# A new order for the steps of a fused retention and SwiGLU kernel, from its second up stage to its end

## The chip, the cores and the metric

The kernel runs on one core of one Trainium2 chip. The metric is the device time of one execution in microseconds; the time of a kernel is the median of several runs. TensorE (PE in the profile) multiplies, with its weight loads listed apart (PEld); VectorE (DVE), ScalarE (ACT) and GpSimd (POOL) do the elementwise work; SyncE (SP) issues nearly all transfers. Each engine works through its own list of instructions in order and waits on semaphores for the others.

## What is computed

A retention layer (a recurrent form of attention with a decay per head), and behind it a SwiGLU feed-forward block on its output. The sizes are 4 sequences, 8 heads, 768 steps, 64 elements per head, so 3072 tokens of 512 elements; the feed-forward width is 1536. All is float32.

```python
for t in range(S):                       # per sequence and head
    state = gamma * state + outer(k[:, :, t], v[:, :, t])
    y[:, :, t] = scale * (q[:, :, t] @ state)
x = y.transpose(0, 2, 1, 3).reshape(B * S, H * D)
g = x @ w_gate
out = (silu(g) * (x @ w_val)) @ w_out
```

## The kernel before

The tokens go through in four segments, numbered 0 to 3, of 2 x 384 tokens each. A segment has an up stage (x times w_gate and w_val, and the gate) and a down stage (the gated values times w_out). While segment s is in its stages, the retention of segment s+1 is done between the products, in chunks, as many small products of 64 rows and columns: `mm`, line 824, called from `scores_of` (or `scores_of1`), `low`, `old` and `grow`.

Precision: each float32 operand is split into three pieces that TensorE takes in its fast float32 form. The first piece is made on ScalarE, the second on VectorE, the third on GpSimd or VectorE; one block of products is then a series over the pieces.

The up stages 1 to 3 (`up3`, `product`, line 1229) use a scheme of Strassen's kind: for each of the 12 blocks f of the width, seven products p0 to p6 of six matmuls of 384 columns each, in four banks of PSUM, and ten small steps u0 to u9 between them that copy a bank out (u0, u3, u4 on ScalarE, lines 1244 to 1246), add (VectorE, lines 1244 to 1247) and apply the gate. A product that adds to a bank must wait until a step has taken out what it held: p2 of a block waits for u0.

The down stages (`down`, line 1298) have 12 blocks of six products, one for each 128 tokens, each of three matmuls of 512 columns. The weights of a block (`w_load`, line 1277, tile oitem, 768 KB) come into one of three slots, so a load can be issued only when the block three places ahead is through.

The retention of a segment goes by pairs p = 0, 1, 2 of chunks. The inputs come with `load_pair` (lines 815 and 819; one such load is up to four transfers). The scores go into banks, VectorE multiplies them with the decay mask (line 846), ScalarE scales k with the decays (line 857), TensorE mixes (`mix2`), ScalarE copies the results out into chunk_x (line 1159), and VectorE adds the new state to the old (line 923).

The order of all this is written out by hand in one list, `PLAN` (lines 51 to 235): each word is a step, with the number of the segment ahead of the slash. `run` calls the steps in this order, and since each step emits its instructions when it is called, the list fixes the order on every engine and in every queue. The names that the prediction uses:

- s/pF.N product N of block F in the up stage of segment s; s/uF.N its small steps
- s/wF.G.K piece K (0 on ScalarE, 1 on VectorE, 2 on GpSimd or VectorE) of group G of the weights of block F
- s/WF load of the down weights of block F; s/DF.T down product for tokens T; s/eT and s/oT its closing copy and store
- s/lN load N of the retention's inputs (5 to a pair: k, q, v and k, q by rows); s/scP scores of pair P; s/AP and s/BP the two mixings of pair P; s/kP.N scaling of k; s/yP.ZR copies of results; s/newP.Z adding to the state

The set `ELSE` (lines 236 to 245) names the steps that go to the other engine than usual: a third piece of weights (line 1134) goes to VectorE if it is in the set and to GpSimd if not, and a closing copy e changes between ScalarE and VectorE (lines 1327 and 1329).

```python
def run():
    for key in PLAN.split():
        if key in events:
            events.pop(key)[2]()
        else:
            do(key)
...
def either(step):
    return both if step in ELSE else pool
```

Of the kernel before, what the change touches and what calls it, by code (L numbers as in the profile page):

```python
# [113 lines left out]
    1/w3.2.0 1/u2.0 1/p2.2 1/u2.3 1/w1.2.2 1/p1.6 1/w3.0.1 1/w2.2.2 1/u2.1 1/w3.0.2 1/L4 0/o1 1/u1.8
    0/o4 2/tc 1/L5 1/p2.3 1/p2.4 1/u2.4 1/p2.5 0/e3 0/e5 2/tb 1/w4.1.0 1/w4.0.0 1/w3.2.1
    1/u1.9 1/p3.0 1/u3.0 1/w3.1.1 2/R 1/L6 1/u2.5 1/p2.6 1/u2.6 1/u1.2 1/w3.1.2 1/p3.3 1/u3.4
    1/u2.8 1/w4.0.1 1/u2.9 1/w4.0.2 1/u1.7 1/p3.2 1/u3.3 1/w4.1.1 1/p3.1 1/u3.1 1/p4.0 1/p3.4 1/p3.5
    1/w4.1.2 1/u3.6 1/u3.5 1/p4.1 1/w5.1.0 1/w5.1.1 1/u4.0 1/p4.2 1/w5.0.0 1/w4.2.0 1/w5.2.0 1/w5.2.1 1/w5.2.2
    1/w4.2.1 1/p4.3 1/u4.3 1/p4.4 1/w5.0.1 1/u2.2 1/u4.4 1/w3.2.2 1/p3.6 1/w6.2.0 1/p4.5 1/u3.8 1/u4.5
    1/u2.7 1/w6.1.0 1/w4.2.2 1/w6.0.0 1/p4.6 1/u4.8 1/u3.9 1/w5.0.2 1/p5.0 1/u3.2 1/u4.1 1/u4.2 1/u5.0  # L120
    1/p5.1 1/u4.6 1/p5.2 1/w5.1.2 1/p5.3 1/u5.3 1/u5.4 1/p5.4 1/L7 0/o5 2/l0 1/p5.5 1/w7.1.0
    1/w7.0.0 1/w6.1.1 1/w6.0.1 1/u4.9 1/u5.1 1/u4.7 1/u3.7 1/w6.2.1 1/u5.5 1/u5.6 1/w6.2.2 2/cv1 1/w7.0.1
    1/w6.0.2 1/p6.0 1/p5.6 1/u6.0 2/cv3 1/u5.8 1/u5.9 1/p6.1 1/u6.1 1/w7.1.1 1/p6.2 1/w6.1.2 1/p6.3
    1/L8 1/w7.2.0 1/u6.3 1/p6.4 1/L9 1/u6.4 1/u6.5 2/td 1/w8.2.0 1/p6.5 1/w8.1.0 1/w8.0.0 1/p6.6
    1/u6.8 0/o3 1/w7.0.2 1/w7.1.2 1/u6.6 1/p7.3 1/u7.4 1/u5.2 1/u6.2 1/w8.2.1 1/w7.2.1 1/L10 1/w8.2.2
    1/w8.0.1 1/u6.9 1/w8.1.1 1/p7.0 1/u7.0 1/p7.1 1/u7.1 1/u5.7 1/p7.2 1/u7.3 1/w8.0.2 1/p8.0 1/u8.0
    1/u7.2 1/w9.2.0 1/p7.4 1/p7.5 1/u7.6 1/w9.1.0 1/w9.0.0 1/p8.1 1/u8.1 1/w9.2.1 1/u7.5 1/w9.0.1 1/w9.1.1
    1/p8.2 1/w8.1.2 1/p8.3 2/cv0 1/u8.3 1/u8.4 1/w7.2.2 1/p7.6 1/u7.8 1/u7.9 1/w10.2.0 1/L11 2/l3
    2/k0.2 2/k0.0 1/p8.5 1/p8.4 1/w10.2.1 1/u8.5 1/w9.1.2 1/w10.1.0 1/w9.0.2 1/p9.0 1/u9.0 1/w10.0.0 1/p9.1
    1/w10.1.1 1/u8.6 1/w9.2.2 1/u7.7 1/w10.0.1 1/w10.0.2 1/p8.6 1/w11.2.0 2/k0.3 1/p9.2 1/u9.3 1/u8.8 1/w11.2.1  # L130
    1/w11.2.2 1/w10.2.2 2/l1 2/sc0 2/l6 1/p9.3 1/u9.4 1/p9.4 1/p9.5 1/w11.1.0 1/w11.0.0 2/cv2 2/dec0.1
    1/u8.9 1/u9.5 1/p9.6 1/u9.1 1/u6.7 1/u9.2 1/u9.6 2/l4 1/p10.0 1/w11.0.1 1/w11.0.2 1/w11.1.1 1/W0
    2/l2 1/u9.8 2/k0.1 1/u10.0 2/l10 2/l5 1/w10.1.2 1/w11.1.2 1/u9.9 1/p10.1 1/p10.3 1/u10.4 1/p10.2
    1/u8.2 1/u10.3 1/p10.5 1/p10.4 1/h0.0 1/u10.6 2/q0.0 1/p11.3 1/p11.0 1/h1.0 1/u10.5 1/p10.6 1/h0.1
    1/u10.1 1/h0.2 1/u9.7 1/u11.0 1/p11.2 1/p11.1 1/u10.8 1/u11.3 1/u11.4 1/p11.4 1/h1.1 2/l9 1/u10.9
    1/p11.5 1/u11.1 1/u8.7 1/u10.2 1/u11.2 1/u11.5 1/p11.6 1/u11.6 1/D0.1 1/u10.7 2/dec0.0 1/D0.2 1/u11.8
    1/u11.9 2/A0 2/new0.0 2/sc1 1/h1.2 1/u11.7 1/D0.3 1/W1 1/D1.3 1/D1.1 2/dec1.0 2/dec1.1 1/D0.4
    1/D0.5 1/D0.0 1/D1.5 1/D1.0 2/cm 2/was0.10 2/mv0.0 2/was0.11 2/y0.01 1/h2.0 1/h4.0 1/h2.1 2/y0.00
# [11 lines left out]
    1/W9 1/h11.0 2/L0 1/D8.4 1/D8.5 2/new2.0 2/mv2.0 2/was2.11 2/x1.0.2 1/h9.2 1/D9.2 2/x1.0.1 1/h11.1  # L150
    1/h11.2 2/y2.00 2/was2.10 2/B2 2/y2.10 2/sum2.2 2/y2.11 2/sum2.0 2/sum2.1 1/D9.1 1/D9.4 1/D9.5 1/W10
    1/D9.0 1/D10.1 1/D9.3 1/W11 1/D11.1 1/D10.3 1/D10.4 2/L2 1/D10.2 1/D10.5 1/D11.4 1/D10.0 1/D11.5
    2/w0.0.0 2/w0.0.1 2/sum2.3 2/x2.1.0 2/new2.1 2/w0.0.2 2/x2.0.0 2/x2.0.2 3/was0.01 2/x2.1.1 2/w0.1.0 2/w0.2.0 2/x2.2.0
    2/x2.2.1 2/x2.2.2 2/w0.2.1 2/x2.0.1 2/x2.1.2 2/w0.1.1 2/L3 2/w0.1.2 1/D11.0 1/e0 2/w1.0.0 2/w1.0.1 1/e1
    1/o1 2/w1.2.0 2/w1.2.1 2/w1.2.2 1/o0 1/D11.2 1/D11.3 2/p0.0 2/u0.0 2/w1.1.0 2/p0.1 2/w0.2.2 2/w1.1.1
    2/w1.1.2 2/L4 2/p0.2 2/u0.3 2/w2.1.0 2/p0.3 2/p0.4 2/u0.4 2/p0.5 2/w2.0.0 2/u0.1 2/u0.5 1/e2
    2/w1.0.2 2/w2.0.1 2/p0.6 2/u0.8 2/u0.9 2/w2.0.2 2/p1.0 2/u1.0 2/p1.1 2/p1.2 2/u0.6 2/p2.0 2/p1.3
    2/w3.1.0 2/w3.1.1 2/u1.1 2/w2.1.1 2/u1.3 2/p1.4 2/w2.2.0 2/u2.0 2/w2.2.1 2/p2.1 1/e3 2/w3.2.0 2/u1.4
    2/u1.5 2/p1.5 2/u1.6 2/w2.2.2 2/u0.2 2/w3.0.0 2/w3.0.1 2/u0.7 2/p2.2 2/u2.3 2/p1.6 2/u1.8 2/u1.9
    2/w2.1.2 2/w3.0.2 2/p2.3 2/u2.4 2/p2.4 2/p2.5 2/w4.1.0 2/w4.0.0 2/u2.1 2/u2.5 2/p2.6 2/u2.8 2/u2.6  # L160
    2/w4.0.1 2/w4.0.2 2/u2.9 2/w4.2.0 2/p3.0 2/u3.0 2/p3.1 2/w4.1.1 2/w4.1.2 2/L5 2/p3.2 2/u1.2 2/u3.3
    2/u3.1 2/w3.1.2 2/p3.3 2/u2.2 2/p3.4 2/u3.4 2/p3.5 2/w5.1.0 2/w5.2.0 2/u1.7 2/w3.2.1 2/w3.2.2 2/u3.5
    2/w5.2.1 2/w5.2.2 2/p4.0 2/u4.0 2/u3.2 2/w5.1.1 2/w4.2.1 2/p3.6 2/u3.8 2/w5.0.0 2/w5.1.2 2/p4.1 2/L6
    2/p4.2 2/u3.6 2/u3.9 2/u4.3 2/p4.3 2/u4.4 2/p4.4 2/p4.5 2/w6.1.0 2/w5.0.1 2/u4.1 2/w5.0.2 2/p5.0
    2/u5.0 2/u4.6 2/u4.5 2/p5.3 2/w6.2.0 2/u5.4 2/w6.1.1 2/p5.1 2/p5.2 1/e4 2/w6.0.0 2/w6.0.1 2/u5.1
    2/L7 2/p5.5 2/u5.3 2/u5.6 2/p5.4 2/w7.1.0 2/w4.2.2 2/p4.6 2/w7.2.0 2/u4.8 2/w7.0.0 2/w6.1.2 2/u5.5
    2/w7.2.1 2/u3.7 2/u5.2 2/u4.9 2/u2.7 2/u4.2 2/w6.2.1 2/u5.7 2/p5.6 2/u5.8 2/w6.0.2 2/p6.1 2/p6.0
    2/u6.0 2/p6.3 1/o3 2/u6.4 2/p6.2 2/u6.3 2/p6.5 2/L8 1/o2 3/l3 3/k0.0 2/L9 2/p6.4
    2/w6.2.2 2/u4.7 2/w7.0.1 2/w7.0.2 2/u5.9 2/p7.0 2/w7.1.1 2/L10 2/u6.5 2/u6.6 1/e5 2/w8.2.0 1/o5
    2/w8.2.1 2/u6.1 2/w8.1.0 2/w8.0.0 2/w8.0.1 2/w8.1.1 2/L11 1/o4 3/l0 2/w8.2.2 2/mv2.1 2/u7.0 2/p6.6  # L170
    2/w7.1.2 2/p7.3 2/u7.4 2/p7.2 2/u7.3 2/p7.5 2/u7.6 2/u6.8 2/u6.9 2/u6.2 2/p7.1 2/p7.4 2/w9.1.0
    2/w9.0.0 2/w9.2.0 2/u7.5 2/w8.0.2 2/p8.0 2/u7.1 2/u8.0 2/w9.0.1 2/w9.1.1 2/w9.1.2 3/l1 2/w9.0.2 2/w9.2.1
    2/w7.2.2 2/p7.6 2/u7.8 2/w8.1.2 2/p8.3 2/p8.2 2/u8.4 2/p8.5 2/u8.3 2/u8.6 2/p8.4 3/k0.3 2/w10.1.0
    2/u6.7 2/u8.5 2/p9.3 2/u9.4 2/u7.2 2/u7.9 2/p8.1 2/p9.0 2/p8.6 2/u8.1 2/u9.0 2/p9.2 2/u7.7
    2/w10.0.0 2/w10.0.1 2/u8.8 2/w10.1.1 3/l4 2/w10.0.2 2/u8.9 2/p9.5 2/p9.1 2/u9.3 2/p9.4 3/k0.1 2/p10.0
# [1319 lines left out]
```

## Time and profile before

| | us |
|---|---|
| median of three runs | 640.45 |
| lowest and highest run | 640.33, 642.25 |
| the profiled execution | 641.82 |
| its span, first to last instruction | 639.95 |

The profile is of one further execution. Its span is the time between the first and the last instruction on the core, and 1.87 us of its time lie around that. In the views, a row of a timeline has its start, its length, engine, line, operation, output and inputs and the number of instructions, and behind them in brackets how long the engine was idle before and what released it; "issue" is time in which the profile shows nothing that the engine waited for. The rows of stretches have for each engine its busy time and in brackets its number of instructions. Queue 8 carries TensorE's instructions into the core, in packets. The granted clock of TensorE is 1.00 in every stretch but the last.

The stages lie in the span like this: the first up stage to about 105 us, the down stages of segments 0, 1 and 2 from about 105 to 196, 286 to 347 and 437 to 500 us, the up stages of segments 1, 2 and 3 between and behind them, and the last down stage from about 587 us.

### The profile page before, as it was taken

The numbers are of one execution on the slowest core, as the hardware profiler recorded it, in microseconds if no ns is written. First come the engines' busy times: TensorE is split into PE (matmuls) and PEld (weight loads), VectorE is DVE, ScalarE is ACT, GpSimd is POOL, SyncE is SP. The second block draws the span as 40 slices with busy tenths as digits, with TensorE's granted clock in tenths as the row PEclk, the third lists the DMA queues.
The fourth block names the chain that finished last, engine by engine and source line by source line (L and its number), as shares of the span: only waits on it lengthen the run. The fifth ranks groups of instructions, "written<-read, shape, count | busy, mean of one in ns | idle before, by whom it ended". The sixth has DMA issues, their size and how long they took to land.

```text
span 639.9 us, 14128 instructions
## 1 busy us (share of the span) xinstructions
PE 632.4 (99%) x5587; PEld 582.4 (91%) x5587; DVE 502.3 (78%) x759; ACT 397.2 (62%) x845; POOL 181.8 (28%) x121
## 2 busy tenths in 40 slices
...
GB/s 319 276 347 332 366 319 277 276 319 304 257 283 304 181 148 188 144 249 218 295 239 182 129 125 188 198 189 192 240 376 168 166 115 116 178 32 145 214 197 149
DMA packets 57747, 143.03 MB, mean 224 GB/s; under 512 B 5840, under 2 KB 28368, under 8 KB 57680
## 3 DMA queue, kind: packets, MB, share of 16 engines
...
q8 instruction: 44, 0.72, 0.5%
...
## 4 chain that ended last, share of the span: by engine, by line
PE 92%; DMA 3%; ACT 3%; issue 1%; DVE 1%; SPq 0%; ACTq 0%
PE bank L1229 40%; PE bank L1298 28%; PE bank L1056 13%; PE bank L824 5%; PE bank L1074 3%; DMA hT<-in_k_n_dram 2%; PE bank L650 1%; DMA hT<-in_k_t_dram 1%; ACT states L915 1%; PE bank L741 1%; PE bank L727 1%; PE bank L712 1%; ACT hT L857 1%; ACT local L870 0%; PE bank L691 0%
## 5 line engine op out<-in xcount | busy, mean ns | idle before, releaser
L1298 PE MATMUL bank<-oitem,gitem 128*128 128x512 f32 x867 | 205.2, 393 | 0.0
L1298 PEld LDWEIGHTS bank<-oitem,gitem 128*128 128x128 f32 x867 | 160.3, 188 | 34.5 <-DVE tmp L955 0.4
L1229 PE MATMUL bank<-xa,gitem 128*128 128x384 f32 x864 | 159.6, 335 | 0.2 <-ACT tmp L1244 0.2
L1229 PEld LDWEIGHTS bank<-xa,gitem 128*128 128x128 f32 x864 | 150.5, 188 | 0.9 <-ACT tmp L1244 0.5
L1134 POOL TENSOR_TENSOR gitem<-gitem 128x768 fp32r<-128x768 f32 x42 | 81.6, 1948 | 149.1 <-DVE gitem L1131 128.4
L1134 POOL TENSOR_TENSOR oitem<-oitem 128x512 fp32r<-128x512 f32 (+1 forms) x46 | 52.7, 1148 | 188.8 <-DVE oitem L1131 151.8
L1056 PE MATMUL bank<-xa,oitem 128*128 128x384 f32 x480 | 84.2, 335 | 0.0
L1229 PE MATMUL bank<-xb,gitem 128*128 128x384 f32 x432 | 83.5, 334 | 0.0
L1056 PEld LDWEIGHTS bank<-xa,oitem 128*128 128x128 f32 x480 | 83.0, 188 | 0.2
L1131 DVE SCALAR_TENSOR_TENSOR gitem<-gitem,loads 128x768 fp32r<-128x768 f32 x72 | 74.6, 1048 | 7.7 <-ACT gitem L1128 6.2
L417 DVE SCALAR_TENSOR_TENSOR gitem<-gitem 128x768 fp32r<-128x768 f32 x78 | 77.5, 1002 | 2.2 <-DVE gitem L1131 0.5
L1229 PEld LDWEIGHTS bank<-xb,gitem 128*128 128x128 f32 x432 | 75.8, 188 | 0.2
L1128 ACT ACTIVATE gitem<-loads 128x768 fp32r<-128x768 f32 x72 | 59.3, 844 | 23.2 <-PE bank L1229 18.7
L1128 ACT ACTIVATE gitem<-hT 128x768 fp32r<-128x768 f32 x48 | 39.8, 841 | 39.9 <-PE bank L1298 31.2
L1131 DVE SCALAR_TENSOR_TENSOR gitem<-gitem,hT 128x768 fp32r<-128x768 f32 x48 | 46.2, 962 | 22.3 <-ACT gitem L1128 22.1
L1229 PE MATMUL bank<-xb,oitem 128*128 128x384 f32 x216 | 43.2, 335 | 0.0
L1229 PEld LDWEIGHTS bank<-xb,oitem 128*128 128x128 f32 x216 | 38.0, 188 | 0.1
L1246 ACT COPY tmp<-bank 128x384 f32<-128x384 f32 x36 | 17.3, 481 | 25.0 <-PE bank L1229 22.6
L1246 DVE TENSOR_TENSOR hT<-bank,tmp 128x384 f32<-128x384 f32 x36 | 20.0, 554 | 16.0 <-PE bank L1229 15.2
L1245 ACT COPY tmp<-bank 128x384 f32<-128x384 f32 x36 | 17.3, 480 | 23.0 <-PE bank L1229 17.2
L1244 ACT COPY tmp<-bank 128x384 f32<-128x384 f32 x36 | 17.2, 478 | 21.3 <-PE bank L1229 14.2
L1247 DVE TENSOR_TENSOR hT<-bank,tmp 128x384 f32<-128x384 f32 x36 | 19.9, 552 | 10.6 <-PE bank L1229 10.5
...
## 6 DMA issues: line engine op xcount, KB each, us to landing
...
```

Of the source, the lines that this page charges most:

```text
L417: stt(o, x, 1.0, y, op0=mul, op1=op)
L824: nc.tensor.matmul(o, a, b, start=start, stop=True, skip_group_check=True)
L1056: nc.tensor.matmul(o, w[:, a, ts(b, P)], X0[:, a, i, NC - 1 - b], start=a == b == 0, stop=a == 2 and b == NC - 1, skip_group_check=True)
L1074: nc.tensor.matmul(o, w[:, a, ts(b, P)], X0[:, a, :, NC - 1 - b, ts(j, P)], start=a == b == 0, stop=a == 2 and b == NC - 1, skip_group_che ...
L1128: act(o[0], x, AF.Copy, scale=CUT / FAR)
L1131: stt(o[1], f32(o[0]), -FAR, x, op0=mul, op1=add)
L1134: op(o[2], f32(o[0]), f32(o[1]), op=add)
L1229: nc.tensor.matmul(o, w[:, a, k], x[:, a, KH - 1 - k], start=start and a == k == 0, stop=a == 2 and k == KH - 1, skip_group_check=True)
L1245: lambda: act(gate, c11, AF.Silu, scale=ONE), lambda: copy(u2, x),
L1246: lambda: copy(p5, wb), lambda: tt(h1, x, p5, op=add),
L1247: lambda: tt(h0, wb, u2, op=add), lambda: tt(h0, h0, gate, op=mul),
L1298: nc.tensor.matmul(banks[tok][:, cols], hs[f][:, a, ds(i * TH + u * P, P)], wo[f][:, a, cols], start=f == a == 0, stop=f == NF - 1 and a = ...
```

## The change

The list has the same 2369 words. The first 759 stay; from the 760th on, in the closing of the first down stage and the start of the second up stage, all are in a new order. The set `ELSE` is another: 39 third pieces of weights in it where there were 44, so that five more go to GpSimd, and seven closing copies change their engine. Nothing else changes: the same products, the same transfers, the same tiles. The diff, cut to the places that are spoken of:

```diff
@@ PLAN, start of the second up stage @@
-    0/e2 0/o2 1/x2.2.1 1/w0.1.1 1/p1.1 1/x2.2.2 2/ta 1/u0.3 1/w1.1.0 1/u1.0 1/p1.2 1/w0.2.1 1/w0.2.2
+    0/e2 0/o2 1/x2.2.1 1/w0.1.1 1/p1.1 2/ta 2/tb 2/R 1/x2.2.2 1/u1.0 1/u0.3 1/p1.2 0/e1
...
+    2/cv0 1/w1.2.0 1/w1.1.0 1/w0.1.2 1/w0.2.1 1/w0.2.2 1/p0.3 1/u0.4 1/w2.1.0 1/p0.4 1/p0.5 1/w2.0.0 1/w1.1.1
+    1/u0.5 1/p0.6 1/u0.6 1/u1.3 1/w2.2.0 1/u0.8 1/w1.1.2 1/p1.3 1/u1.4 1/w1.2.1 1/L3 1/L4 1/w2.0.1
...
@@ second down stage @@
-    2/new0.1 2/l7 1/W2 1/W3 1/D2.2 1/D2.0 1/D2.3 1/D2.1 2/l8 2/k1.1 1/h4.2 1/D2.5 1/D2.4
-    2/l11 2/l14 1/D3.0 1/D3.3 1/D3.5 1/D3.1 1/D3.2 1/D3.4 2/q1.0 1/h5.1 1/h5.2 2/sum0.0 2/sum0.1
-    2/k1.0 2/mv0.1 2/k1.2 1/h6.0 2/k1.3 2/q1.1 2/A1 1/W4 1/D4.2 1/D4.1 1/D4.3 2/was1.01 2/was1.00
...
-    1/D6.5 2/y1.10 2/k2.1 2/y1.11 2/x1.2.0 2/new1.1 2/sc2 2/x1.1.0 1/W7 1/W8 1/D6.0 1/D6.1 1/D6.4
...
+    2/mv0.0 2/B0 2/l7 2/l8 1/D2.2 1/W3 2/new0.1 1/D2.1 1/D2.3 1/D3.2 2/l11 1/D3.1 1/D2.4
...
+    2/x0.0.0 2/new1.0 2/x0.2.2 1/h5.2 2/y1.01 2/l14 1/W4 1/W5 1/D4.3 1/D4.5 1/D4.1 1/D4.2 1/D5.3
+    1/D5.5 1/D4.0 1/D4.4 2/mv1.0 1/D5.1 2/was1.10 2/y1.00 2/B1 2/was1.11 1/h7.0 1/h8.0 2/y1.11 2/x0.0.1
...
+    2/l10 2/y1.10 1/h8.1 1/h8.2 1/h7.1 1/h7.2 2/k2.2 2/new1.1 2/sc2 2/was2.00 2/x1.2.0 2/k2.1 1/W7
...
@@ end of the third up stage @@
-    3/begin 2/u11.1 2/u11.6 3/dec0.0 2/D0.1 2/D0.0 2/u11.8 2/u11.9 3/A0 3/l6 3/l9 3/l5 3/sc1
...
+    3/l9 2/u11.3 2/w10.2.2 2/p10.6 3/sc1 2/W1 3/l11 2/u10.8 2/p11.4 2/u11.4 2/p11.5 2/h2.0 2/p11.1
...
+    2/u11.1 2/D0.0 2/D0.2 2/h1.2 2/u11.8 2/u11.2 2/u11.9 3/k0.2 3/A0 3/y0.01 3/y0.00 3/dec1.1 3/dec1.0
...
@@ ELSE @@
-    "0/e1", "0/e3", "0/e4", "0/e5", "1/e2", "1/e3", "1/e5",
...
+    "0/e1", "0/e3", "0/e5", "1/e1", "1/e3", "1/w0.0.2", "1/w0.1.2",
...
```

More of the change, by code (lines that the diff above doesn't have):

```diff
@@ L114 @@
[L114 to L138, printed above, removed]
@@ L150 @@
[L150 to L175, printed above, removed]
@@ L186 @@
-    3/k1.2 3/k1.3 3/q1.0 3/sum0.1 3/sum0.3 3/x0.0.0 2/h3.2 2/D2.5 3/k1.1 2/h5.1 3/x0.0.1 2/h6.0 3/x0.1.1
-    2/W3 2/D3.4 3/l7 2/W4 3/k1.0 2/h6.1 2/D3.5 2/D3.3 3/x0.2.2 3/A1 3/new1.0 3/was1.11 3/y1.00
-    2/D3.1 2/D4.1 2/D3.0 2/D4.0 2/D4.3 2/D3.2 2/D4.2 3/mv1.0 3/y1.01 3/B1 3/y1.10 3/x0.0.2 2/h5.2
-    2/D4.4 2/D4.5 3/l13 3/l14 2/W5 2/D5.4 2/D5.5 2/D5.1 2/D5.3 2/D5.2 2/D5.0 3/was1.10 3/new1.1
-    3/y1.11 3/l11 3/sc2 3/x1.1.0 3/sum1.0 3/sum1.1 3/sum1.3 3/x1.1.1 3/k2.3 2/h7.0 2/h8.0 3/sum1.2 3/x1.0.0
@@ new lines @@
+    2/sc1 1/h1.2 1/D1.2 1/D0.0 1/D1.0 1/h2.1 2/dec1.0 2/dec1.1 1/D0.4 1/D0.5 1/D1.1 2/y0.01 1/h4.0
+    1/u11.2 1/u11.7 1/D0.3 1/h4.1 1/h2.2 2/l9 2/tc 2/y0.00 2/was0.10 2/td 2/q0.0 1/h4.2 2/q1.1
+    2/q0.1 2/q1.0 1/h3.0 1/D1.5 1/D1.3 1/D1.4 2/was0.11 1/h5.0 1/h3.1 1/h3.2 1/W2 1/D2.5 1/D2.0
+    2/mv0.0 2/B0 2/l7 2/l8 1/D2.2 1/W3 2/new0.1 1/D2.1 1/D2.3 1/D3.2 2/l11 1/D3.1 1/D2.4
+    1/D3.5 2/mv0.1 2/k1.1 2/y0.11 2/y0.10 2/k1.0 2/sum0.0 2/sum0.1 1/h5.1 2/sum0.3 2/was1.00 2/k1.3 2/k1.2
+    1/D3.0 1/D3.4 2/A1 1/D3.3 2/sum0.2 1/h6.0 2/begin 2/x0.2.0 2/x0.2.1 2/x0.1.0 2/x0.1.2 2/x0.1.1 2/was1.01
@@ new lines @@
+    2/x0.0.0 2/new1.0 2/x0.2.2 1/h5.2 2/y1.01 2/l14 1/W4 1/W5 1/D4.3 1/D4.5 1/D4.1 1/D4.2 1/D5.3
+    1/D5.5 1/D4.0 1/D4.4 2/mv1.0 1/D5.1 2/was1.10 2/y1.00 2/B1 2/was1.11 1/h7.0 1/h8.0 2/y1.11 2/x0.0.1
+    1/D5.2 1/W6 1/D5.0 1/D5.4 1/h6.1 1/h6.2 1/D6.0 1/D6.3 1/D6.2 1/D6.1 1/D6.5 1/D6.4 2/l13
+    2/l10 2/y1.10 1/h8.1 1/h8.2 1/h7.1 1/h7.2 2/k2.2 2/new1.1 2/sc2 2/was2.00 2/x1.2.0 2/k2.1 1/W7
+    1/D7.5 1/D7.0 1/D7.2 1/D7.1 2/x1.2.1 2/x0.0.2 2/sum1.2 2/q2.0 2/sum1.0 2/dec2.0 1/D7.3 2/k2.3 2/x1.1.0
@@ new lines @@
+    2/D0.4 2/D0.5 2/u11.7 2/D0.3 2/W2 2/W3 2/D1.3 3/l7 2/D1.2 2/D1.5 2/h3.0 2/D1.1 2/D1.0
+    2/D1.4 2/W4 2/h4.1 3/new0.0 3/mv0.0 3/B0 3/l14 2/h4.2 2/h2.2 2/h3.1 2/D2.3 3/k1.1 3/k1.3
+    2/h5.0 3/k1.0 3/y0.10 3/was0.10 3/y0.11 3/was0.11 2/D2.2 2/D2.4 2/D2.1 2/D2.5 2/h5.1 2/h5.2 3/q1.1
+    3/new0.1 3/mv0.1 3/was1.00 3/k1.2 2/D2.0 2/h3.2 2/D3.1 3/q1.0 3/A1 2/D3.2 2/D3.0 2/D3.3 2/D3.4
+    2/D4.1 2/D4.2 2/D3.5 2/D4.4 2/D4.3 2/D4.5 3/x0.1.0 3/x0.1.1 3/sum0.0 3/sum0.2 3/was1.01 3/x0.2.0 3/new1.0
```

178 lines of the change are left out of this document (109 added, 69 removed).

## The prediction

> **What bounds the kernel now.** I read the page first: the span, the busy share of each engine and the chain that ended last.
>
> ```profile
> span 639.9 us, 14128 instructions
> PE 632.4 (99%) x5587; PEld 582.4 (91%) x5587; DVE 502.3 (78%) x759; ACT 397.2 (62%) x845; POOL 181.8 (28%) x121
> q8 instruction: 44, 0.72, 0.5%
> PE 92%; DMA 3%; ACT 3%; issue 1%; DVE 1%; SPq 0%; ACTq 0%
> ```
>
> TensorE is busy for 632.4 of 639.9 us, and the change leaves its 5587 product records as they are: only their order moves. So what can be won is idle time of PE and edges between kinds of products, nothing else. The line of queue 8 gives the size of an instruction packet: 5587 products and as many weight loads in 44 packets are 254 instructions each, that is 127 products with their loads. Next, where PE idles, in stretches that follow the stages (us, then busy time and records of PE, PEld, DVE, ACT, POOL, then clock, DMA share and GB/s):
>
> ```profile
> 105.00:196.00 91.00, 90.95 (x1126) 77.19 (x1127) 81.44 (x116) 67.94 (x170) 38.03 (x24) 1.00 0.83 286
> 196.00:286.00 90.00, 89.78 (x573) 88.97 (x572) 73.01 (x115) 56.52 (x119) 36.95 (x23) 1.00 0.59 190
> 286.00:347.00 61.00, 60.86 (x884) 49.75 (x883) 49.41 (x77) 40.87 (x109) 1.90 (x1) 1.00 0.76 235
> 347.00:437.00 90.00, 90.00 (x575) 89.45 (x574) 71.42 (x115) 55.98 (x112) 29.39 (x19) 1.00 0.52 172
> 437.00:500.00 63.00, 62.40 (x896) 51.40 (x895) 50.75 (x79) 37.99 (x98) 1.20 (x1) 1.00 0.70 236
> 500.00:587.00 87.00, 87.00 (x500) 86.56 (x499) 70.46 (x107) 49.45 (x95) 31.66 (x20) 1.00 0.38 127
> ```
>
> The second up stage starts near 196 us, and the two orders are the same until a little after that, so the first 196 us stay. From there to 587 us PE is idle 0.22 + 0.14 + 0.60 us, in one place in each of three stretches. A product's record reaches past the start of the next one, so the loss at each place is larger than its idle time; I take it from pairs of like groups.
>
> **The wait for a packet, near 443.7 us.** The same view for the small products of the retention (line 824) alone, PE and PEld:
>
> ```profile
> 438.52:441.01 2.49, 2.49 (x160) 2.42 (x160) 1.00 0.98 400
> 443.29:445.67 2.38, 1.78 (x96) 1.58 (x96) 1.00 0.20 62
> 456.80:458.36 1.56, 1.56 (x96) 1.49 (x96) 1.00 0.73 185
> 319.82:321.36 1.54, 1.40 (x64) 1.20 (x64) 1.00 0.85 311
> 147.23:148.32 1.09, 1.09 (x64) 1.02 (x64) 1.00 1.05 414
> 181.50:182.95 1.45, 1.40 (x64) 1.20 (x64) 1.00 1.04 424
> ```
>
> A group of 96 records takes 1.56 us undisturbed and 2.38 us here: 0.82 us lost. The timeline says that no other engine held it, and the DMA view of 441 to 443 us has one packet of queue 8:
>
> ```profile
> 443.29 0.45 PE L824 MATMUL bank<-tab,loads 64*64 64x64 f32 x15
> 444.34 0.47 PE L824 MATMUL bank<-tab,loads 64*64 64x64 f32 x17 [0.60 <-issue]
> ...
> q8 instruction: 1, 0.02, 4.3%
> ```
>
> In front stand 160 records in 2.49 us, then only nine large products: a packet's worth of instructions is used up in about 4 us. In the new order the scores of pair 1 of the last stage (3/sc1, 64 records) leave the mixing 3/A0 (96 records) and go some 6 us ahead, into the up products. Counted in the two orders of TensorE's instructions: of the 155 products between the asking for a packet and the end of what is already in, 143 are small at this place; in the new order the densest place behind 196 us has 124 and takes 8.4 us, and nothing in the old order that had 7.2 us or more lost time. The group at 181.50 (138 small, 6 us; 1.45 against 1.09 us) lies ahead of the change and stays. So I take 0.82 us off; bounds 0 (rival a) and 0.82.
>
> The Trainium skill (Runtime: NRT & Kernel Launch, section Instruction fetch mechanics) says that instructions come in blocks of 16 KiB holding 256 and that the fetch is hidden because dispatch is slower than the filling. By that rule the 0.82 us would be 0; the 0.60 us of "issue" above speak against it here.
>
> **The wait for ScalarE, near 202 us.**
>
> ```profile
> 200.16 0.30 ACT L774 COPY local<-local 64x128 f32<-64x128 f32 x1
> 200.48 0.48 ACT L1245 COPY tmp<-bank 128x384 f32<-128x384 f32 x1
> 200.99 0.85 ACT L1128 ACTIVATE gitem<-loads 128x768 fp32r<-128x768 f32 x1
> 201.74 0.46 ACT L1244 COPY tmp<-bank 128x384 f32<-128x384 f32 x1
> 202.25 0.82 PEld L1229 LDWEIGHTS bank<-xa,gitem 128*128 128x128 f32 x5 [0.54 <-ACT tmp L1244]
> 202.25 0.97 PE L1229 MATMUL bank<-xa,gitem 128*128 128x384 f32 x4 [0.22 <-ACT tmp L1244]
> ```
>
> The product 1/p1.2 adds to a bank that 1/u1.0 (L1244) first copies out, and ScalarE does 1/u0.3 and a 0.85 us weight split (1/w1.1.0) before that copy. The new list has 1/u1.0 ahead of both: it can run as soon as its product is done, about 1 us earlier, and the wait goes. PE idles 0.22 us, the loads 0.54; since loads otherwise follow one another without a gap I take 0.50. What is late next is 1/w1.1.0, by about half a microsecond; its product 1/p1.3 now stands five products later, so it is covered; without that cover it would cost its delay, 0.5 us.
>
> **The wait for VectorE, near 320 us.** The group 2/sc2 at 319.82 took 1.54 against 1.09 us, 0.45 lost. The chain of waits of that stretch leads back to a load:
>
> ```profile
> 309.04 9.13 DMA hT<-in_k_n_dram
> ...
> 318.25 0.40 ACT hT L857
> ...
> 319.80 0.43 DVE states L923
> ```
>
> The four loads of k for pair 2 (2/l13) take 9.13 us. ScalarE's scaling 2/k2.2 waits for them, the copies 2/y1.10 and 2/y1.11 (chunk_x) stand behind it, and VectorE's 2/new1.1, which frees the bank that the scores need, waits for those. In the new list both copies stand ahead of the first 2/k2.*, so a late load no longer holds them. I take 0.45 off; bounds 0 and 0.45. What is late next is 2/k2.* itself, whose load now has 8.2 us for 9.2; the products that need it come a whole group later, and uncovered it costs what the load is late, some 1 us.
>
> **What the split adds.** One group of 160 becomes 64 and 96, one of them among up products:
>
> ```profile
> 263.83 1.20 PE L1229 MATMUL bank<-xb,oitem 128*128 128x384 f32 x6
> 264.87 1.20 PE L1229 MATMUL bank<-xa,gitem 128*128 128x384 f32 x6
> 266.01 1.16 PE L824 MATMUL bank<-loads,chunk_x 64*64 64x64 f32 x64
> 267.10 3.40 PE L1229 MATMUL bank<-xa,gitem 128*128 128x384 f32 x18
> 270.34 1.22 PE L1229 MATMUL bank<-xb,oitem 128*128 128x384 f32 x6
> ```
>
> Six up products take 1.04 us from start to start, 1.14 before the small group, and eighteen behind it 3.24 for 3.12: 0.22 us of edges. Alone, 64 and 96 take 1.09 + 1.56 = 2.65 us, together 2.49: 0.16. The split costs 0.38 us. No other group is split or merged.
>
> **The other edits.** Five more third pieces of weights go from VectorE to GpSimd, and seven of the closing copies change between ScalarE and VectorE. A third piece on GpSimd:
>
> ```profile
> L1134 POOL TENSOR_TENSOR gitem<-gitem x42: 1842/1851/2698, 197.1 to 574.1; 128x768 fp32r<-128x768 f32 x42
> ```
>
> It takes 1.85 us (longest 2.70). By its place in the list the tightest piece has 0.57 us to spare after 1.85 us, at two places, so 0 to 0.28 us each; GpSimd is 28% busy, and I take 0. SyncE's queue moves too: the loads of down weights and of the retention's inputs, and the stores, all keep their number and size. The smallest lead of a down weight is in the second down stage: 1/W4 stands behind 2/l14, four loads that wait for the end of 2/B0 and hold the queue for 0.6 us each:
>
> ```profile
> L819 SPq DMA_DIRECT2D chunk_x<-in_q_t_dram x8: 596/605/1462, 297.7 to 459.7; - x8
> ...
> DMA to landing us min/median/max: 3.5/4.6/9.2
> ...
> DMA to landing us min/median/max: 6.8/7.1/7.5
> ...
> DMA to landing us min/median/max: 9.0/9.0/9.0
> ```
>
> The first line of landings is for all loads of down weights, the second for 1/W4 and 1/W5 (issued at 301.3 and 302.5 us), the third for 1/W6. Counted in the new list, 30 large products (0.227 us each) and one group of 96 stand between the end of 2/B0 and the first product with 1/W4: 8.6 us, less 2.4 us of issuing, 6.2. If it lands in 6.8 us as before PE loses 0.6. In the old order the loads of k and an up weight ran beside it; in the new one they are issued earlier or later, so I take a landing of 6.2 or less, no loss; bounds 0 and 0.6.
>
> **The sum.** 0.82 + 0.50 + 0.45 - 0.38 = 1.39 us. The profiled execution took 641.82 us with a span of 639.95; less 1.39 it is 640.4. It lies 1.37 us above the median of the runs shown, 640.45. If that median has the same waits it goes to 639.06; I forecast 639.0.
>
> **The rivals.** (a) The change doesn't do what it says: the packet comes in time anyway in executions without a profile. For it: the median is 1.37 us below the profiled time. Against: no trace shown here lacks the 0.60 us. Then 0.50 + 0.45 - 0.38 = 0.57, so 639.9. (The rule of the Trainium skill's page Runtime: NRT & Kernel Launch, cited above, is this case.)
> (b) Clearly faster: the packet at 181.50 (0.36 us) arrives in time too, and small stretches of the up stages go: 500 records in 87.00 us where 1.04/6 each makes 86.7, 0.3; in 347 to 437 us 511 up products and one small group with its edges make 89.87 of 90.00, 0.13. 1.39 + 0.36 + 0.43 = 2.18, so 638.3. For it: the smallest leads between an engine's step and the product that waits for it are a little longer in the new list. Against: the first lies ahead of the change.
> (c) Slower: down weights land too late in the second down stage. Landings of 9.0 us as for 1/W6 cost 1/W4 2.8 us and 1/W5, whose lead is 7.1 us, 1.9: 4.7 us, and the time is 640.45 - 1.39 + 4.7 = 643.8. It decides against the forecast of no clear change from 3.3 us on, a mean landing of 8.3 us. For it: DMA is busy 0.76 in that stretch and three loads in a row took 6.8 to 9.0. Against: the loads of k that shared the queues have moved ahead.
>
> **How the numbers follow.** About 0.3%, 1.9 us, is what a measurement of this kernel can tell from no change (its runs go from 640.33 to 642.25). The forecast has 0.45 and (a) 0.13, both within it: 0.58. (b) has 0.22, (c) 0.20. The range goes from a little under (b), 638.0, to 642.6, inside (c) with one of its two loads late; the forecast's own, by the bounds above, goes from 0.82 + 0.54 + 0.45 - 0.38 = 1.43 us gained to 0.22 - 0.38 - 0.56 - 0.6 = 1.32 lost, 639.0 to 641.8.
>
> **What would show it.** Right: no "issue" idle of PE within a small group behind 196 us; 1/u1.0 ahead of 1/u0.3 on ScalarE and no idle loads near 202 us; PE busy equal to the stretch, to 0.1 us, from 196 to 587; one small group more. Wrong: PE idle behind DMA of oitem near 300 to 310 us, or behind GpSimd's L1134 in an up stage; a packet again late, at a group behind 196 us.

## The result, and the profile after

| | before | changed |
|---|---|---|
| median of 22 runs each, side by side, us | 642.16 | 639.97 |
| lowest and highest, us | 640.33, 644.82 | 639.05, 642.59 |
| span of the profiled execution, us | 639.95 | 637.4 |

The ratio of the times is 0.9973, with a 95% interval from 0.9964 to 0.9982: 1.7 us less (1.2 to 2.3); the two medians lie 2.19 us apart, inside that interval. The forecast was 1.39 us less. The page of the changed kernel, in the parts that answer to those of before (its line numbers are one lower than before's, since the list is one line shorter: 823 is `mm`, 1228 an up product, 1297 a down product):

```profile
span 637.4 us, 14115 instructions
PE 630.0 (99%) x5587; PEld 580.3 (91%) x5587; DVE 499.2 (78%) x753; ACT 396.1 (62%) x846; POOL 191.9 (30%) x126
q8 instruction: 44, 0.72, 0.5%
PE 97%; DMA 2%; DVE 0%; issue 0%; SPq 0%; ACTq 0%; ACT 0%
```

The same 5587 products and the same 44 packets, five instructions more on GpSimd, and "issue" at 0% in the chain that ended last, where it had 1%. The stretches behind 196 us in the changed kernel (busy time and instructions of PE, PEld, DVE, ACT, POOL, then clock, DMA share, GB/s):

```profile
196.00:286.00 90.00, 90.00 (x580) 88.93 (x582) 73.27 (x112) 57.93 (x122) 39.20 (x25) 1.00 0.58 184
286.00:347.00 61.00, 61.00 (x889) 50.45 (x888) 49.77 (x78) 41.24 (x108) 0.95 (x1) 1.00 0.73 240
347.00:437.00 90.00, 90.00 (x632) 89.19 (x631) 75.35 (x114) 53.67 (x112) 32.91 (x21) 1.00 0.55 180
437.00:500.00 63.00, 62.96 (x838) 51.56 (x837) 48.00 (x76) 38.35 (x98) 5.16 (x3) 1.00 0.72 230
```

PE idled 0.22 + 0.14 + 0.60 us in these stretches before, and 0.04 us now; that bit is new, near 473 us, where the loads of TensorE wait 0.47 us for a down weight. The small products of the four groups that the prediction speaks of, and of the one at 180 us that it left as it is:

```profile
320.72:321.81 1.09, 1.09 (x64) 1.02 (x64) 1.00 0.97 289
430.58:431.67 1.09, 1.09 (x64) 1.02 (x64) 1.00 0.64 191
438.14:439.70 1.56, 1.56 (x96) 1.49 (x96) 1.00 1.17 236
446.06:447.62 1.56, 1.56 (x96) 1.49 (x96) 1.00 1.12 260
180.30:181.76 1.46, 1.41 (x64) 1.20 (x64) 1.00 1.03 420
```

How much of the difference between the two profiled executions lies behind the place where the orders part? From the first up product of segment 1 to the end of the last down product, first in the kernel before, then in the changed one:

```profile
196.64 1.57 PE L1229 MATMUL bank<-xb,gitem 128*128 128x384 f32 x8
...
629.74 6.54 PE L1298 MATMUL bank<-oitem,gitem 128*128 128x512 f32 x31
```

```profile
195.43 2.27 PE L1228 MATMUL bank<-xb,gitem 128*128 128x384 f32 x12
...
629.65 4.04 PE L1297 MATMUL bank<-oitem,gitem 128*128 128x512 f32 x20
```

Before: 636.28 - 196.64 = 439.64 us; changed: 633.69 - 195.43 = 438.26. The changed part is 1.38 us shorter. The other 1.21 us lie ahead of 196 us, where the two kernels are the same, and belong to the one execution, not to the change.

### The profile page after: what moved, and what is told of

Same layout as the page of the kernel before. It is cut to its first block, busy times and chain, and to the rows that moved or that the text cites. A ratio compares the mean times of both kernels' runs of the same rounds, so it can differ in the third digit from the quotient of the medians.

```text
span 637.4 us, 14115 instructions
## 1 busy us (share of the span) xinstructions
PE 630.0 (99%) x5587; PEld 580.3 (91%) x5587; DVE 499.2 (78%) x753; ACT 396.1 (62%) x846; POOL 191.9 (30%) x126
## 4 chain that ended last, share of the span: by engine, by line
PE 97%; DMA 2%; DVE 0%; issue 0%; SPq 0%; ACTq 0%; ACT 0%
PE bank L1228 41%; PE bank L1297 32%; PE bank L1055 13%; PE bank L823 6%; PE bank L1073 3%; DMA hT<-in_k_t_dram 1%; DMA hT<-in_q_t_dram 1%; PE bank L649 1%; PE bank L726 1%; PE bank L740 1%; PE bank L711 0%; DVE tmp L655 0%; DVE chunk_x L1320 0%; SPq L483 0%; ACTq L483 0%
## 5 line engine op out<-in xcount | busy, mean ns | idle before, releaser
L1133 POOL TENSOR_TENSOR gitem<-gitem 128x768 fp32r<-128x768 f32 x45 | 88.2, 1965 | 254.0 <-DVE gitem L1130 220.9
L1133 POOL TENSOR_TENSOR oitem<-oitem 128x512 fp32r<-128x512 f32 (+1 forms) x48 | 55.9, 1167 | 71.2 <-DVE oitem L1130 47.0
L416 DVE SCALAR_TENSOR_TENSOR gitem<-gitem 128x768 fp32r<-128x768 f32 x75 | 74.6, 1002 | 1.9 <-DVE gitem L1130 0.5
L1244 ACT COPY tmp<-bank 128x384 f32<-128x384 f32 x36 | 17.3, 480 | 24.8 <-PE bank L1228 22.7
L1245 DVE TENSOR_TENSOR hT<-bank,tmp 128x384 f32<-128x384 f32 x36 | 19.9, 553 | 16.3 <-PE bank L1228 11.9
L1247 DVE TENSOR_TENSOR hT<-hT,bank 128x384 f32<-128x384 f32 x36 | 19.8, 550 | 13.0 <-ACT bank L1247 12.8
L1243 ACT COPY tmp<-bank 128x384 f32<-128x384 f32 x36 | 17.1, 476 | 18.8 <-PE bank L1228 14.4
```

Source lines behind the costliest of these rows:

```text
L416: stt(o, x, 1.0, y, op0=mul, op1=op)
L1133: op(o[2], f32(o[0]), f32(o[1]), op=add)
L1244: lambda: act(gate, c11, AF.Silu, scale=ONE), lambda: copy(u2, x),
L1245: lambda: copy(p5, wb), lambda: tt(h1, x, p5, op=add),
L1247: lambda: act(x, x, AF.Silu, scale=ONE), lambda: tt(h1, h1, x, op=mul))
```

## The experiments

Each is a small edit of one of the two kernels; "b" stands for the kernel before, "a" for the changed one. A ratio is to the kernel before, run on the same chip at the same time, with its 95% interval.

**One wait at a time, in the old order.** b_y1 has the copies of results ahead of the scaling that waits for a load:

```diff
-1/h8.1 2/l13 2/k2.2 1/D6.5 2/y1.10 2/k2.1 2/y1.11
+1/h8.1 2/l13 2/y1.10 2/y1.11 2/k2.2 1/D6.5 2/k2.1
```

> The old order with 2/y1.10 and 2/y1.11 ahead of the first 2/k2.*. Theory: the small group 2/sc2 near 320 us takes 1.09 us instead of 1.54, the others stay; 0.45 us less, ratio 0.9993. Rival (the late load of k matters for the products, not only for the copies behind it): the group stays long, or the mixing of pair 2 waits some 0.5 us later, ratio 1.0000.

Measured 0.9993 (0.9977 to 1.0009), which can't be told from 1. The trace can tell more. Small products in b_y1, the scores 2/sc2 and then 3/B0:

```profile
318.92:320.01 1.09, 1.09 (x64) 1.02 (x64) 1.00 0.49 175
441.94:443.85 1.91, 1.78 (x96) 1.57 (x96) 1.00 0.12 34
```

2/sc2 takes 1.09 us where it took 1.54: this wait is gone, as said. 3/B0, not touched here, lost only 0.35 us to its packet, where the prediction read 0.82. Still the changed part, measured as above, takes 439.97 us, 0.33 more than before: near 474 us products wait 0.33 and 0.21 us for a load of v, and near 476 us 0.17 for a down weight, at a place where nothing was moved.

b_u10 has 1/u1.0 early, but ahead of 2/ta as well:

```diff
-1/x2.2.2 2/ta 1/u0.3 1/w1.1.0 1/u1.0 1/p1.2
+1/x2.2.2 1/u1.0 2/ta 1/u0.3 1/w1.1.0 1/p1.2
```

> The old order with one step moved: 1/u1.0 ahead of 1/u0.3 and 1/w1.1.0. Theory (three separate waits make the gain): the idle of the weight loads near 202 us (0.54 us) goes, the waits near 320 and 443.7 us stay; about 0.50 us less than before, ratio 0.9992. Rival (ScalarE is late there for a longer reason, and the next step on it is late instead): the wait comes back at 1/p1.3 or another product within 10 us, and the time stays at 1.0000.

Measured 1.0016 (1.0001 to 1.0031): slower. ScalarE and TensorE in its timeline:

```profile
200.98 0.48 ACT L1244 COPY tmp<-bank 128x384 f32<-128x384 f32 x1 [1.53 <-PE bank L1229]
201.49 0.93 ACT L774 COPY local<-local 64x128 f32<-64x128 f32 x3
...
203.99 0.58 ACT L1329 ACTIVATE chunk_x<-bank 128x512 f32<-128x512 f32 x1
...
204.62 3.39 PE L1229 MATMUL bank<-xa,gitem 128*128 128x384 f32 x18 [1.59 <-ACT chunk_x L1329]
```

1/u1.0 (L1244) waits 1.53 us at the head of ScalarE's queue for its product. The copies of 2/ta (L774), which ran in that time before, now run behind it, and so does the closing copy 0/e1 (L1329), which frees the bank of 1/p0.3. The wait of 0.22 us is gone and one of 1.59 us has come. The two waits that this edit doesn't touch are larger in this profile: 2/sc2 loses 0.85 us (1.94 for 1.09) and 3/B0 1.04 (2.60 for 1.56).

b_sc1 takes the scores 3/sc1 away from 3/A0, with their loads and the mask ahead of them, and b_all3 makes all three moves:

```diff
-3/sc0 2/p10.4 ... 3/dec0.1 3/k0.2 ... 2/p11.4 2/h1.1 ... 3/dec0.0 ... 3/A0 3/l6 3/l9 3/l5 3/sc1
+3/sc0 3/l6 3/l5 2/p10.4 ... 3/dec0.1 3/dec0.0 3/k0.2 ... 2/p11.4 3/sc1 2/h1.1 ... 3/A0 3/l9
```

> The old order with the scores 3/sc1 ahead among the up products, their two loads 3/l5 and 3/l6 right behind 3/sc0 and 3/dec0.0 behind 3/dec0.1. Theory (packet): the 0.60 us of issue at 443.7 us goes, since the densest place there now lasts 8.1 us; the split costs 0.38; 0.44 us less, ratio 0.9993. Rival (the wait belongs to the products of 3/B0 themselves): it stays at 0.6 us, and with the split the time is 0.4 us more, ratio 1.0006.

> The old order with these three edits together. Theory: 1.39 us less, ratio 0.9978, and PE without idle time between 196 and 587 us but for the 0.1 us edges; within 0.3 us of the new order. Rival (the new order gains by more than these waits, for instance by longer leads everywhere): at most 0.7 us less, ratio 0.9989 or more, while the new order measured 0.9973.

Measured 1.0006 (0.9989 to 1.0024) and 1.0024 (1.0008 to 1.0040): no gain, and a loss. First what b_sc1 waited for, with its group 3/B0, then b_all3:

```profile
308.96 7.78 PE L1298 MATMUL bank<-oitem,gitem 128*128 128x512 f32 x33 [1.29 <-DMA oitem<-wdnt]
...
444.13:446.16 2.03, 1.99 (x96) 1.76 (x96) 1.00 0.03 8
```

```profile
439.49 1.16 PE L824 MATMUL bank<-chunk_x,loads 64*64 64x64 f32 x64 [1.95 <-DMA loads<-in_k_t_dram]
```

The "issue" wait is gone in b_sc1. But 3/B0 still loses 0.47 us (2.03 for 1.56): the 1.09 us of scores no longer stand between 3/A0 and it, and its products come while ScalarE is still copying the state that they read. In b_all3 the scores come before their load of k (1.95 us), and b_u10's wait is there again. The 1.29 us in b_sc1 are at a place that this edit doesn't touch; more on that below.

**The scores put back in the new order.**

```diff
-2/p10.6 3/sc1 2/W1 ... 3/k0.2 3/A0 3/y0.01
+2/p10.6 2/W1 ... 3/k0.2 3/A0 3/sc1 3/y0.01
```

> The new order with 3/sc1 put back right behind 3/A0, so one group of 160 again. If the wait at 443.7 us came from the group of 160 as such: it is back, 0.82 us, less the split's 0.38; 0.44 us slower than the new order, ratio to before 0.9980. Theory (it is the phase of the packets against the small products): in the new order a packet is not asked for there, the densest window lasts 7.6 us, no issue idle, and the saved split makes it 0.38 us faster than the new order, ratio 0.9967.

Measured 1.0001 (0.9988 to 1.0014): the whole gain is lost, more than either theory gave. But the reason is not the packet:

```profile
441.83 1.29 DVE L846 TENSOR_TENSOR tmp<-bank,local 128x512 f32<-128x512 f32 x2 [2.85 <-PE bank L824]
...
443.18 1.21 PE L1298 MATMUL bank<-oitem,gitem 128*128 128x512 f32 x4 [1.41 <-DVE tmp L846]
```

The down product behind the group takes a bank that the mask on VectorE (L846) must first read out; with the scores late, that is 1.41 us late (another product, near 436 us, waits 0.40 us for VectorE). In the new order that product (2/D0.4) stands right behind the group; in the old one four other down products and 3/B0 stand ahead of it.

**Other packet borders, the same order.** 16 tiny products on a tile of zeros, behind the warm-up at the start, move every later border of a packet 64 instructions forward and change nothing else in the order:

```diff
-    warm_up(8)
+    warm_up(8); [nc.tensor.matmul(banks[3][:64, :64], warm[:64, :64], warm[:64, :64], start=True, stop=True, skip_group_check=True) for _ in range(16)]
```

> The old order with the same 64 instructions more at the start, nothing moved. Theory (packets): the group near 181 us takes 1.09 us instead of 1.45; the window near 437 us shrinks from 4.1 to 2.4 us, so the idle at 3/A0, 3/sc1 or 3/B0 grows from 0.8 to 2 us or more; a further packet falls into a window of 5.7 us near 314 us. Together 1 to 1.5 us slower than before, ratio 1.0020. Rival (no packets): all groups as before, time as before or 0.5 us more.

> The new order with 16 tiny products (64 instructions) more at the very start, where PE waits for the first load; they compute nothing that is used. They shift all packets by a quarter. Theory (packets): the wait of 0.36 us in the small group near 181 us, which the change left, goes, and none comes; 0.3 us faster than the new order, ratio 0.9968. Rival (that group waits for something else): it still takes 1.45 us, and the time is that of the new order or 0.5 us more for the added products.

Measured 1.0074 (1.0049 to 1.0100) in the old order and 0.9985 (0.9965 to 1.0005) in the new one. In b_shift64 the group of 160 (3/A0 and 3/sc1), then 3/B0, the group near 181 us, the stop itself, and the 3 us behind it:

```profile
439.29:445.09 5.80, 2.76 (x160) 2.60 (x160) 1.00 0.60 216
448.91:450.47 1.56, 1.56 (x96) 1.49 (x96) 1.00 0.57 162
182.34:183.43 1.09, 1.09 (x64) 1.02 (x64) 1.00 1.05 434
...
444.82 0.34 PE L824 MATMUL bank<-chunk_x,loads 64*64 64x64 f32 x7 [3.04 <-issue]
...
445.00:448.00 3.00, 3.00 (x14) 2.35 (x11) 2.75 (x4) 0.29 (x2) 0.00 (x0) 0.51 0.02 5
```

This is the plainest proof of the packet wait. With the border elsewhere, the wait leaves 3/B0 and the group at 182 us, both whole now, and comes in the group of 160: 5.80 us for 2.49, of which 3.04 us are idle. The 155 products that the prediction counts from the asking to the running out took 2.8 us here in the trace, and 4.5 us at the old place. In the 3 us behind the stop the granted clock is 0.51, and the nine matmuls of the down stage there take 3.82 us where they took 2.28. So the loss is larger than was expected (1.0020): the changed part is 4.34 us longer than before's, 2.49 of it in the groups of 160 and 96 and 1.54 in those nine matmuls.

The traces also show the border itself. The views put seven stops of PE down to "issue", in six profiles (before, b_u10, b_all3, b_fix, and both with the shift, b_shift64 twice). Counted with its loads and all else that the traces list for TensorE, exactly 2497, 3777 or 8385 instructions of TensorE lie ahead of each, in the shifted kernels with the 64 added ones among them, and the gap in the loads of 3/B0 in b_y1 lies behind 8385 too. These numbers are 5 and 18 times 256 apart. The packet wait near 181 us is the one behind 3777.

In the new order with the same shift no group behind 196 us is cut. One ahead of it is:

```profile
144.88 0.27 PE L824 MATMUL bank<-tmp,loads 64*64 64x64 f32 x2 [0.69 <-issue]
...
q1 hardware_dynamic: 1036, 2.89, 96.1%
```

The 155 products there took 8.8 us, more than any such window behind 196 us that lost time; but from 136 to 144 us the transfers hold 96.1% of the DMA time, and the packet came late all the same. The group near 181 us, at 187 us here, is whole (1.09 us), as was expected; the ratio can't be told from that of the new order, nor from 1. The tiny products also cost time at the start (2.08 and 3.67 us of PE in the two profiles), so the two ratios are not the packets' alone.

**The set ELSE.** a_else is the changed kernel with the whole old set, a_close with the old sharing of the closing copies only. The old set has five third pieces more than the new one only on balance: the new set gives 26 pieces to GpSimd that were on VectorE and 21 to VectorE that were on GpSimd. So a_else moves 47 of them, not five. The closing copies, as both have them:

```diff
-    "0/e1", "0/e3", "0/e5", "1/e1", "1/e3", ... "2/e3",
+    "0/e1", "0/e3", "0/e4", "0/e5", "1/e2", "1/e3", "1/e5", ... "2/e1", "2/e5",
```

> The new order with the old set of steps on the other engine: the five third pieces go back to VectorE, the seven closing copies to their old engines. Theory (these edits cost and bring nothing): as the new order, ratio to before 0.9973 within 0.0010, no new idle of PE over 0.3 us. Rival (part of the gain is the relief of VectorE): PE waits for VectorE in an up stage, 0.5 us or more, ratio 0.9981 or more.

> The changed kernel with the old sharing of the closing copies alone (which of ScalarE and VectorE scales a finished block of the output); the third pieces of the weights stay shared as in the new set. The whole old set made the changed kernel 5.2% slower, with waits of TensorE for third pieces on VectorE and GpSimd (12.1 + 4.6 + 3.4 us). Theory (the third pieces make it, since they stand where the other engine's queue has no room; the closing copies are 0.6 us each and hidden): ratio 0.9973, as the changed kernel, within 0.001. Rival (the closing copies matter as well: one that changes engine holds the queue in front of an evacuation): a wait of 0.5 us or more for ScalarE or VectorE beside a closing copy (L1329, L1325), ratio 0.998 to 1.01.

Measured 1.0524 (1.0499 to 1.0550) for a_else, some 34 us over the kernel before and 35 over the changed one, and 1.0004 (0.9994 to 1.0015) for a_close, which loses the whole gain. The waits of PE in a_else (total, times, longest) and its second up stage; then a_close:

```profile
PE bank L1229 <- DVE gitem L417: 12.1, 5, 3.6
PE bank L1229 <- POOL gitem L1134: 4.6, 2, 3.5
...
196.00:286.00 90.00, 79.82 (x471) 77.33 (x470) 61.91 (x93) 46.18 (x96) 33.50 (x20) 0.91 0.44 148
```

```profile
502.17 3.39 PE L1229 MATMUL bank<-xa,gitem 128*128 128x384 f32 x18 [1.07 <-ACT chunk_x L1329]
```

A third piece (L417 on VectorE, L1134 on GpSimd) in the wrong queue is late by up to 3.6 us, and behind such waits the clock falls: its mean is 0.91 in that stage and 0.979 in the whole execution. The waits sum to 21 us; the lower clock makes some 14 us more (an estimate: 2.1% of the span of 676.4). The closing copies matter too: one that goes back to ScalarE stands behind an evacuation there, and the product that wants its bank waits 1.07 us. The theory for a_close fell, its rival holds.

**Room for what is displaced.** b_fix makes the three moves in the old order once more: 1/u1.0 behind 2/ta, 3/sc1 two up products later than in b_sc1, 3/B0 three down products later. b_fixL also takes a load of up weights out from between the down weights. b_fix2 answers the two waits that b_fix had:

```diff
 b_fix
-2/ta 1/u0.3 1/w1.1.0 1/u1.0 1/p1.2
+2/ta 1/u1.0 1/u0.3 1/w1.1.0 1/p1.2
-3/mv0.0 3/B0 2/D1.2 3/dec1.0 3/dec1.1 2/D0.4 2/D0.5
+3/mv0.0 2/D1.2 3/dec1.0 3/dec1.1 2/D0.4 2/D0.5 3/B0
 b_fixL, on top
-1/h6.1 2/L1 1/W6 ... 2/sc2 2/x1.1.0
+1/h6.1 1/W6 ... 2/sc2 2/L1 2/x1.1.0
 b_fix2, on top of b_fix
-1/u0.3 1/w1.1.0 1/p1.2 ... 1/w1.2.0 0/e1 1/p0.3
+1/u0.3 0/e1 1/w1.1.0 1/p1.2 ... 1/w1.2.0 1/p0.3
-2/D0.5 3/B0 ... 3/sum0.2 3/l8 ... 3/x0.0.0 2/h3.2
+3/B0 2/D0.5 ... 3/sum0.2 2/h3.2 3/l8 ... 3/x0.0.0
```

> The three moves in the old order again, each now with room for what it displaced: 1/u1.0 goes between 2/ta and 1/u0.3 (2/ta's 0.94 us of copies stay ahead of it and fill ScalarE's wait), the scores 3/sc1 go behind 2/p11.6 and not 2/p11.4 (some 2 us more for the load of k that was 1.9 us late), and 3/B0 goes three down products later (the window from asking for the packet to running out becomes 8.1 us by count, and VectorE's and ScalarE's steps have time). Theory (three waits, one split, the sizes add up): the waits near 202, 320 and 443 us are gone, no other wait of over 0.3 us takes their place, and the gain is 0.82 + 0.50 + 0.45 - 0.38 = 1.39 us: ratio 0.9978, span measured from the first product of the second up stage 1.4 us shorter than in the kernel before. Rival (the old order has no room: each wait removed comes back elsewhere): ratio 1.000 or above and a new wait of 1 us or more in the trace.

> b_fix with one more step moved: the load of an up weight (2/L1, 896 KB) that the old order issues between the down weights 1/W5 and 1/W6 goes behind 2/sc2. In five kernels with the old order around it, TensorE waited 0 to 1.3 us near 309 us for a down weight. Theory (that load shares the queues with the down weights, and the new order gains by having none there): the three down weights issued from 296 to 309 us land in 6.5 us or less (7.5 in the kernel before, 8.8 in b_sc1, 6.0 in the changed kernel), no wait near 309 us, ratio 0.0003 to 0.0010 below that of b_fix (0.2 to 0.6 us, the mean of that wait). Rival (the loads of q and k alone make them late): landings stay at 7.5 us or more and the ratio is that of b_fix.

> b_fix with its two new waits answered: the closing copy 0/e1 (L1329), for whose bank TensorE waited 0.53 us at 204 us, goes ahead of the weight split 1/w1.1.0 (0.85 us on ScalarE) that had pushed it, and the third piece 2/h3.2 on VectorE, which ended 9 us after 3/B0 where the moved 3/B0 left 7.6 us of down products, goes 2.0 us of VectorE's work earlier, with 3/B0 two and not three down products later. Theory (a wait that is removed is worth its size once all that the move displaces has room; b_fix failed by these two alone): no wait of over 0.3 us between 196 and 587 us, excess time of TensorE from 196 us on 1.4 to 1.8 us less than in the kernel before, ratio 0.9970 to 0.9985, as the changed kernel. Rival (the old order is tight at every engine: new waits come as often as they are answered): another wait of 0.5 us or more, ratio 0.999 to 1.003.

Measured 1.0024 (1.0014 to 1.0034) for b_fix, 1.0036 (1.0023 to 1.0048) for b_fixL, 0.9998 (0.9986 to 1.0009) for b_fix2. The groups near 182 us, of 2/sc2, 3/A0 and 3/B0 in b_fix, and its waits:

```profile
181.70:183.77 2.07, 1.41 (x64) 1.20 (x64) 1.00 0.80 326
320.83:321.92 1.09, 1.09 (x64) 1.02 (x64) 1.00 0.87 265
440.43:441.99 1.56, 1.56 (x96) 1.49 (x96) 1.00 1.05 392
446.33:447.89 1.56, 1.56 (x96) 1.49 (x96) 1.00 0.52 164
...
204.40 3.40 PE L1229 MATMUL bank<-xa,gitem 128*128 128x384 f32 x18 [0.53 <-ACT chunk_x L1329]
...
456.91 1.89 PE L1298 MATMUL bank<-oitem,gitem 128*128 128x512 f32 x7 [1.47 <-DVE gitem L417]
```

The packet wait and VectorE's wait are gone. In their place a closing copy is late by 0.53 us, and the third piece 2/h3.2 (L417) by 1.47. VectorE's work on 3/B0's results runs without a gap into that piece and ends 9 us behind 3/B0, as in the kernel before; by count that left 0.6 us there, and 3/B0 is now three down products, that is nine matmuls or 2.0 us, later. b_fix2:

```profile
290.94 5.73 PE L1298 MATMUL bank<-oitem,gitem 128*128 128x512 f32 x24 [1.03 <-DMA oitem<-wdnt]
458.74 0.97 PE L824 MATMUL bank<-tmp,hT 64*64 64x64 f32 x32 [0.84 <-ACT hT L857]
...
456.01 1.06 ACT L1137 ACTIVATE xa<-tmp 128x1024 fp32r<-128x1024 f32 x1 [0.84 <-DVE tmp L417]
...
201.62 4.17 PEld L1229 LDWEIGHTS bank<-xa,gitem 128*128 128x128 f32 x24
```

Now all three waits of the old order are gone, that near 202 us too (the loads run through it). But the piece put earlier on VectorE delays a sum that ScalarE waits for (0.84 us, L1137), the scaling of k (L857) stands behind that, and TensorE waits 0.84 us at 458.74. The other 1.03 us are a late down weight, at a place where nothing was moved. By the ratios b_fix's loss of 1.5 us came back, but in the traces the changed part of b_fix2 is 441.01 us, 1.37 longer than before's, where 1.4 to 1.8 less was expected: the rival holds.

b_fixL settles nothing. The three down weights landed in 6.7 us (median), a little above the 6.5 expected, where the eight kernels with the old order there had 7.0 to 8.8, and no product near 309 us waited. But the ratio isn't lower than b_fix's. The longest of these landings, b_sc1's, and, with no up weights between, the changed kernel's (transfers of 297 to 309 us: number, KB each, median us from issue to landing):

```profile
oitem<-wdnt SPq DMA_DIRECT2D x3, 768.0 KB, 8.8
```

```profile
oitem<-wdnt SPq DMA_DIRECT2D x3, 768.0 KB, 6.0
```

The load of up weights may carry a part of the difference; how much, stays open.

## Why the prediction was right, and where it was wrong

**The sum.** 1.39 us were predicted, the two traces differ by 1.38 us in the changed part, and the runs by 1.2 to 2.3 us. The loads of TensorE in the changed kernel near the former wait for ScalarE, and ScalarE itself:

```profile
198.41 2.09 PEld L1228 LDWEIGHTS bank<-xb,gitem 128*128 128x128 f32 x12
200.49 4.17 PEld L1228 LDWEIGHTS bank<-xa,gitem 128*128 128x128 f32 x24
...
199.81 0.48 ACT L1243 COPY tmp<-bank 128x384 f32<-128x384 f32 x1 [0.56 <-PE bank L1228]
200.19 0.49 ACT L1244 COPY tmp<-bank 128x384 f32<-128x384 f32 x1
200.56 0.62 ACT L1328 ACTIVATE chunk_x<-bank 128x512 f32<-128x512 f32 x1
```

1/u1.0 (L1243) goes ahead of 1/u0.3 (L1244), the loads have no gap, and 0/e1 (L1328) follows at once, before any weight split: just the step that b_u10 and b_fix had left behind. The twelve products ahead of the former wait and the 24 behind it took 2.47 + 4.28 us from start to start before and take 2.08 + 4.16 now: 0.51 less, where 0.50 was said. The packet's 0.82 and VectorE's 0.45 us are read off the groups above. The split costs what was said: the six up products ahead of the lone 3/sc1 take 1.14 us, the twelve behind it 2.19, 0.10 and 0.11 more than the 1.04 for six of the prediction makes, and the groups 0.16:

```profile
431.67 2.35 PE L1228 MATMUL bank<-xa,gitem 128*128 128x384 f32 x12
433.86 1.20 PE L1228 MATMUL bank<-xb,gitem 128*128 128x384 f32 x6
```

So each of the four terms is there at its size, 1.41 us in all. That the sum fits the traces to 0.01 us is luck: some 0.3 us are lost anew near 473 us (two matmuls there take 0.77 us from start to start, undisturbed ones 0.45), and small differences in other groups make up for it.

**The absolute time** was 1 us too low, 639.0 for 639.97, though the difference fits. The step that failed is "it lies 1.37 us above the median of the runs shown": of three runs two were low. Over 22 runs the kernel before has 642.16, and the profiled execution with its 641.82 was a usual one. The forecast of a change of 0.2% from the lower median put it inside 0.3%; the measured 0.27% stands at that bound, and with 22 runs each its interval doesn't reach 1.

**The packet** (rival a): shown, by b_shift64, by the count of instructions ahead of each stop, and by the groups in b_sc1, b_fix and b_fix2. The 0.57 us that rival (a) left of the gain lies outside the 1.2 to 2.3 us of the runs. The Trainium skill (Runtime: NRT & Kernel Launch, section Instruction fetch mechanics) has the fetch hidden behind dispatch; the 3.04 us in b_shift64 are against it. Three things in that step were wrong. 0.82 us is one draw: 3/B0 in the old order lost 0.82 in the profile of before, 0.35 in b_y1 and 1.04 in b_u10. "Nothing in the old order that had 7.2 us or more lost time" is a fact of that trace and no bound: 8.8 us did not do in a_shift64, where the DMA was full. And of the 155 products ahead of the stop the trace has 146 small ones, not 143, which changes nothing.

**"The other edits": taken at 0**, and no wait of TensorE for them is seen in the changed kernel. But the term was misread: "five more third pieces" is a balance, and 26 went one way and 21 the other. The reason given, that GpSimd is 28% busy and the pieces have time to spare by their places, doesn't carry it either. The new order needs its own sharing: the old set costs 35 us in it, and the closing copies alone, 0.6 us each, cost 2 us. What the new set would do in the old order wasn't run. That a copy is short and ScalarE only 62% busy says nothing of what stands behind the copy.

**Rival c** (late down weights in the second down stage) had the right place and the wrong side. In the changed kernel no product waits for a down weight in that stage; 1/W4 and 1/W5 landed in 5.0 and 6.0 us, within the 6.2 that the forecast assumed. In the old order TensorE waited 0.2 to 1.3 us near 309 us in four of eight profiles with that part unchanged. That the new order gains by it too is likely; it wasn't shown by itself.

**Rival b**: the packet wait at 180 us stayed (1.46 us for 1.09), as the line against it said.

**What the prediction did not see** is how little a single wait is worth by itself. It priced three waits as if each could be taken out alone, and the sum came out since the whole list behind them had been set anew. Taken out by hand in the old order they were gone in the trace, but not in the time: b_y1's 0.45 us is less than its runs can tell and comes back in its trace as late loads, and each of the other moves delayed a step elsewhere by 0.5 to 2 us. Why loads at places that nothing touched came late in b_y1, b_sc1 and b_fix2 stays open.
